# A planned MoE kernel on one core: other orders of the steps in a unit, and GpSimd additions that wait for VectorE sums

## The chip, the cores and the metric

The kernel runs on one core of a Trainium2 chip. The metric is device time in microseconds, the median over runs of the same program; lower is better. The engines are named as in the profile: PE (TensorE matmul), PEld (its weight load), DVE (VectorE), ACT (ScalarE), POOL (GpSimd) and SP (SyncE, which here only starts DMAs).

## The reference

Linear attention with an exponential feature map gives x, 4608 rows of 512 columns. A mixture of eight experts follows; its routing weights P come from eight rounds of row and column normalisation. Only this part is touched by the change:

```python
out = np.zeros((N, D), dtype=np.float32)      # N 4608, D 512
for e in range(E):                            # E 8, F 1024
    h = np.maximum(x @ w1[e], 0.0)
    ye = h @ w2[e]
    out += P[:, e:e + 1] * ye
```

## The kernel before, in words

**Stages.** Attention, routing and expert 0 come first and are not touched. Then experts 1 to 7 follow one another. The 4608 rows are nine groups of 512; x stays in SBUF as xT (bf16) and the result as `acc` (fp32), one tile for each group. Groups are taken in pairs (0,1), (2,3), (4,5), (6,7), and group 8 alone; expert 7 begins with group 8.

**A unit.** For each pair two units are made, one for each value of `fp` (half of the hidden columns); group 8 has one. A unit computes the up product of its own rows, and beside it the down product of an earlier group. Both are done with seven block products in place of eight (Strassen and Winograd's form), so sums of blocks are needed before and after the products:

- Up (`up7`): steps `x1`, `x2`, `x3`, `x4`, `y1`, `w1`, `w2`, each for q = 0 and 1 (`x10` is x1 for q = 0). Each is two wide 128x512 matmuls (L1388) for a pair, and four of 256 columns (L1379) for group 8. `x1` and `x2` are followed by a move, a copy on ACT from one PSUM bank to another (L1447); `w1` by a keep, a copy on ACT to SBUF (L1443); `x3` and `w2` by an addition with relu on DVE (L1450); `y1` and `x4` by a relu on ACT (L1455).
- For pairs of experts 2 to 7 the products x1 and w1 are themselves done with seven inner products: the chains `ia1` to `ia7` (for x1) and `ib1` to `ib7` (for w1), one 128x256 matmul each (L1475). Steps 1 and 2 of a chain are followed by a small copy on ACT (L1484), steps 3 and 4 by a small addition on DVE (`plus`, L1487), which step 4 or 7 of the same chain needs; steps 6 and 7 by the move or keep.
- Down (`down7`): steps `X1`, `X2`, `X3`, `X4`, `Y1`, `Z1`, `Z2`, eight 128x256 matmuls each (L1379). `X1` is followed by a copy to another bank on ACT (L1675). `X2`, `X4` and `Z2` are read by DVE, which adds P times the bank to acc (L1644). `Y1`, `Z1` and `X3` are read by ACT, which scales the bank by P into a buffer V (L1656, two buffers), and POOL adds V to acc (L1659). X1 to X4 use one bank, so that X3 has to be read before X4 begins.
- Sums of blocks are DVE operations on bf16 (L1211): of the weights of each expert (`sums_up`, `inner_sums`, `sums_down`; 128x1024 and 128x256), of the hidden blocks for each down product (`down7`, 128x512), and in expert 1 of x itself (`sums_x`, `inner_x`), which SP stores to DRAM as `xd` and loads again (`X<-xd`) for every later expert. In expert 1 ACT also scales what expert 0 left in acc (L1666).

**What sets the order.** No instruction is issued where it stands in the code. Each call records an `Op` with a cost, its reads and writes; `Plan.schedule` then goes through the recorded operations as a list scheduler: of all operations that are ready it takes the one that can start first, the earlier recorded one on a tie, so the strings `ORDER` and `INNER` set both dependences and priority. The plan holds one more rule: an operation marked `shared` (a DVE sum of blocks, a POOL operation) starts after the last `shared` one has ended (`port`). `Plan.run` then issues the operations in that order, and every engine works through its own in order; across engines only true data dependences are semaphores on the chip. The rule on `shared` lives in the plan alone.

Of the kernel before, what the change touches and what calls it, by code (L numbers as in the profile page):

```python
# [17 lines left out]
class Buf:  # L18


    def __init__(self, ring):
        self.ring, self.t, self.slot, self.left, self.end = ring, None, None, 0, 0.0
        self.last = None
# [91 lines left out]

class Op:
    __slots__ = ("eng", "dur", "lat", "nbytes", "fn", "left", "ready", "users", "idx", "end",
                 "bufs", "deps", "shared", "turn", "unit", "stop", "tiled")

    def after(self, user):  # L120

# [77 lines left out]
class Plan:  # L199
# [3 lines left out]
    def __init__(self):  # L203
        self.last, self.readers = {}, {}
        self.ops = []
        self.prio = 0
        self.port = 0.0

    def op(self, eng, dur, lat, fn, r=(), w=(), takes=(), nbytes=0, shared=False):


        o = Op()
        o.eng, o.dur, o.lat, o.fn, o.nbytes = eng, dur, lat, fn, nbytes
        o.users, o.idx, o.end, o.ready = [], len(self.ops) + self.prio, None, 0.0
        o.shared, o.turn, o.unit, o.tiled = shared, False, 0, 0
        deps = {}
        for key in r:
            for d in self.last.get(key, ()):
                deps[id(d)] = d
        for key in w:  # L220
            for d in list(self.last.get(key, ())) + self.readers.get(key, []):
                deps[id(d)] = d
        bufs = list(takes)
        for key in list(r) + list(w):
            b = key[0] if isinstance(key, tuple) else key
            if isinstance(b, Buf):
                bufs.append(b)
        o.bufs = list({id(b): b for b in bufs}.values())
        for b in o.bufs:
            b.left += 1  # L230
        for key in r:
            self.readers.setdefault(key, []).append(o)
        for key in w:
            self.last[key] = [o]
            self.readers[key] = []
        o.deps = list(deps.values())
        o.left = len(o.deps)
        for d in o.deps:
            d.users.append(o)
        self.ops.append(o)  # L240
        return o

    def start(self, o, free):

        t = max(free, o.ready, self.port if o.shared else 0.0)
        need = {}
        for b in o.bufs:
            if b.slot is None:
                key = id(b.ring.free)
                n = need[key] = need.get(key, 0) + 1  # L250
                at = b.ring.find(n)
                if at is None:
                    return None
                t = max(t, at)
            elif b.last is not None and b.last.eng != o.eng:
                t = max(t, b.last.end)
        return t

    def schedule(self):
        ready = {}  # L260
        free = {}
        links, clock = Links(), Clock()
        for o in self.ops:
            if o.left == 0:
                ready.setdefault(o.eng, []).append(o)
        done = []

        def finish(o):
            for b in o.bufs:
                if b.ring.psum:  # L270
                    b.last = o
                b.left -= 1
                b.end = max(b.end, o.end)
                if b.left == 0:
                    b.ring.give(b.end, b.slot)
            for u in o.users:
                u.left -= 1
                u.ready = max(u.ready, o.after(u))
                if u.left == 0:
                    ready.setdefault(u.eng, []).append(u)  # L280

        while len(done) < len(self.ops) or links.next():
            best = None
            for eng, rq in ready.items():
                f = free.get(eng, 0.0)
                if best is not None and f > best[0]:
                    continue
                for o in rq:
                    t = self.start(o, f)
                    if t is not None and (best is None or (t, o.idx) < best[:2]):  # L290
                        best = (t, o.idx, o)
            landed = links.next()
            if landed and (best is None or landed[0] <= best[0]):
                o = links.land(*landed)
                o.end = landed[0] + 1.0
                finish(o)
                continue
            assert best is not None, "no operation can start"
            at, _, o = best
            ready[o.eng].remove(o)  # L300
            for b in o.bufs:
                if b.slot is None:
                    b.slot = b.ring.take(at)
            dur = clock.takes(at, o.dur, o.tiled) if o.eng == "PE" else o.dur
            free[o.eng] = at + dur
            if o.shared:
                self.port = at + dur
            done.append(o)
            if o.nbytes:
                links.add(o, at)  # L310
            else:
                o.stop = at + dur
                o.end = o.stop + o.lat
                finish(o)
        return done

    def run(self, tc):
        done = self.schedule()
        with tc.manual_schedule():
            for o in done:  # L320
                o.fn()


@with_exitstack
def kernel(
# [159 lines left out]
    def load_w(e, r=()):  # L485
        w1, w2 = new("w1"), new("w2")
        for w, src in ((w1, moe_w1), (w2, moe_w2)):
            dma("POOL", 2 << 20, 280, lambda w=w, src=src: nc.gpsimd.dma_start(
                out=w(), in_=src[e].rearrange("(c p) f -> p c f", p=128)),
                r, [(w, i, j) for i in range(2) for j in range(2)])  # L490
        return w1, w2
# [569 lines left out]
    def stage_g(b):  # L1061
# [4 lines left out]
    at = [0]  # L1066
# [6 lines left out]
    order = (  # L1073
        "lraeaepqbwlqaqawwabwmqlltnrbppnwqbppmrmanbqaqmwwacmpnpbccpwbtcnmqnaqbclupunm"
        "taumquglcapalbcpnqqdcenmucugbblnapmrcqdutabnqpmunpbambccddnqplanmqmducpblttb"
        "augnaqlnrbdcampcadmqeutunqcppmdcaqtdqabpbbmlrqtdnpmuaqualbnagnacctbmqulupran"
        "tdpmtdqcmdnpdabdancpcabbqmpumqbcdgnappqunburqcbugmmnqdcdanumupqbnucmcpnmbddp"
        "bqmpncncubncmmgccg"
    )
# [25 lines left out]
    o = plan.op("X", 0.0, 0.0, swap, w=["late"])  # L1105
# [478 lines left out]
    def down7(e, g, H, B7):  # L1584
# [122 lines left out]


    ORDER = "X1 x10 w10 x11 X2 x20 y10 x21 Z1 y11 X3 w11 x30 x31 x40 x41 w20 Y1 w21 X4 Z2".split()
    INNER = ("ib1 ia1 ia2 ib2 ib3 ia3 X1 Z1 ib5 ia4 ib4 ia5 ia6 ib6 y10 X2 x20 ia7 X3 x21 ib7 "  # L1710
        "x31 y11 w20 x30 Z2 x40 x41 Y1 X4 w21").split()
    END = "X1 p2 Y1 X2 Z1 p3 X3 Z2 X4 p0 p1".split()
    slots, wait = list(range(6)), []

# [20 lines left out]
    for e in range(1, E):  # L1735
        w1, w2 = load_w(e, ["late", ("acc", 4, 0, 0)] if e > 1 else ["late"])
        if e == 1:
            nextX = sums_x(pairs[0])
        A7 = sums_up(e, w1)
        B7 = sums_down(e, w2) if e > 1 else None  # L1740
        turn = [*pairs, (8,)] if e < E - 1 else [(8,), *pairs]
        for n, gs in enumerate(turn):
            X = nextX if e == 1 else load_x(gs)
            H = {g: [] for g in gs}
            for fp in range(len(gs)):
                hs = take()
                for i, z in enumerate(hs):
                    H[gs[min(i, len(gs) - 1)]].append(z)
                un = up7(A7, gs, fp, X, H, ["up0"])
                for o in INNER if ("ia", 1) in un or ("ib", 1) in un else ORDER:  # L1750
                    if o[0] not in "XYZ":
                        un[o[:2], int(o[2])]()
                    elif dn is not None:
                        dn[o]()
                if dn is not None:
                    dn["out"]()
                    slots.extend(dn["slots"])
                if e == 1 and fp == 0 and n:
                    inner_x(turn[n - 1], [(H[gs[0]][0], 0, 1, 1)])
                if e == 1 and fp == 0 and n + 1 < len(turn):  # L1760
                    nextX = sums_x(turn[n + 1], [(H[gs[0]][0], 0, 1, 1)])
                if B7 is None and fp:
                    B7 = sums_down(e, w2)
                if fp == len(gs) - 1:
                    wait += [(e, g, H[g], B7, w2, [z.ring.number for z in H[g]]) for g in gs]
                dn = next_down()
# [35 lines left out]
```

## Time and profile before

| what | value |
|---|---|
| runs, us | 1028.99, 1028.57, 1026.66 (median 1028.57) |
| profiled execution, us | 1027.38 |
| its span, first to last instruction, us | 1025.3 |
| TensorE clock granted | 1.00 |
| DVE busy in the span | 849.4 us (83%) |
| POOL additions L1659 | 186, median 1269 ns, shortest 1260, longest 2078 |
| PE matmul 128x256, mean ns of one | 272 or 273 |
| PE matmul 128x512, mean ns of one | 379 |
| X<-xd loads, median us to landing | 2.7 |
| weight loads on POOL's queue (wx), median us to landing | 12.7 |

How to read it: the span is what the profile shows of one execution, and the time has about 2 us more around it. An expert from 2 on takes some 109 us. Matmuls overlap: the row of one lasts longer than it holds PE, so busy PE in the profile covers a part of each small gap. In a timeline, the bracket at a line's end gives the idle time of its engine before it and the instruction that ended the idle time.

### The profile page before, as it was taken

The numbers are of one execution on the slowest core, as the hardware profiler recorded it, in microseconds if no ns is written. First come the engines' busy times: TensorE is split into PE (matmuls) and PEld (weight loads), VectorE is DVE, ScalarE is ACT, GpSimd is POOL, SyncE is SP. The second block draws the span as 40 slices with busy tenths as digits, with TensorE's granted clock in tenths as the row PEclk, the third lists the DMA queues.
The fourth block names the chain that finished last, engine by engine and source line by source line (L and its number), as shares of the span: only waits on it lengthen the run. The fifth ranks groups of instructions, "written<-read, shape, count | busy, mean of one in ns | idle before, by whom it ended". The sixth has DMA issues, their size and how long they took to land.

```text
span 1025.3 us, 22492 instructions
## 1 busy us (share of the span) xinstructions
PE 1001.4 (98%) x8232; PEld 712.2 (69%) x8232; DVE 849.4 (83%) x1979; ACT 799.8 (78%) x1786; POOL 385.7 (38%) x418
## 2 busy tenths in 40 slices
PE   7899999999999999999999999999999999999998
PEld 4666666644566867787777767786778777786775
DVE  8999989986888997779877887798778977788775
ACT  7999999846878677777777777767776787777874
POOL 5778764400224423343333333333333323323332
PEclk9999999999999999999999999999999999999999
DMA  9999988150113511162116112431126111513343
GB/s 248 193 187 185 175 141 125 34 112 10 48 41 81 122 47 48 47 136 56 48 47 118 40 51 56 82 85 48 47 53 139 47 47 47 109 53 88 135 156 132
DMA packets 115086, 93.94 MB, mean 92 GB/s; under 512 B 54432, under 2 KB 97440, under 8 KB 114976
## 3 DMA queue, kind: packets, MB, share of 16 engines
q1 hardware_dynamic: 83024, 68.46, 26.2%
q0 software_dynamic: 31648, 23.86, 16.5%
q8 instruction: 64, 1.05, 0.4%
q14 instruction: 46, 0.38, 0.1%
q10 hardware_dynamic: 304, 0.20, 0.1%
HBM read 92.62 MB, written 14.55 MB: 105 GB/s over the span
## 4 chain that ended last, share of the span: by engine, by line
PE 91%; DVE 5%; ACT 3%; DMA 1%; issue 1%; SPq 0%; DVEq 0%; ACTq 0%
PE ps L1379 39%; PE ps L1388 24%; PE ps L593 18%; PE ps L1475 7%; PE ps L876 2%; DVE hx L1211 1%; DMA acc<-in_q_dram 1%; DVE hs L1450 1%; ACT k L589 1%; ACT q L589 1%; DVE acc L1644 1%; DVE m L585 0%; ACT hx L1656 0%; DVE hs L1211 0%; DVE wx L585 0%
## 5 line engine op out<-in xcount | busy, mean ns | idle before, releaser
L1659 POOL TENSOR_TENSOR acc<-acc,hx 128x512 f32<-128x512 f32 x186 | 241.9, 1301 | 562.4 <-ACT hx L1656 561.6
L1379 PEld LDWEIGHTS <-hs 128*128 128x128 bf16 x1984 | 193.7, 98 | 59.9 <-issue 2.6
L1450 DVE CUSTOM_DVE_ANT_0 hs<-ps,U 128x512 bf16<-128x512 f32 x252 | 164.7, 684 | 60.6 <-PE ps L1388 57.1
L1644 DVE SCALAR_TENSOR_TENSOR acc<-ps,P,acc 128x256 f32<-128x256 f32 x372 | 163.4, 476 | 40.3 <-PE ps L1379 36.7
L1455 ACT ACTIVATE hs<-ps 128x512 bf16<-128x512 f32 x252 | 151.3, 606 | 57.4 <-PE ps L1388 51.6
L1656 ACT ACTIVATE hx<-ps,P 128x256 f32<-128x256 f32 x372 | 157.8, 479 | 38.5 <-PE ps L1379 34.2
L1379 PEld LDWEIGHTS <-hx 128*128 128x128 bf16 x1488 | 145.5, 98 | 30.5 <-issue 0.2
L1447 ACT COPY ps<-ps 128x512 f32<-128x512 f32 x252 | 146.8, 592 | 25.3 <-PE ps L1475 9.7
L1379 PE MATMUL ps<-hx,hs 128*128 128x256 bf16 x992 | 134.4, 272 | 1.9 <-ACT hx L1656 1.6
L1388 PE MATMUL ps<-X,T 128*128 128x512 bf16 x448 | 131.0, 379 | 1.2 <-DMA X<-xd 1.2
L1388 PEld LDWEIGHTS <-T 128*128 128x128 bf16 x672 | 65.7, 98 | 51.9 <-issue 2.2
L1487 DVE TENSOR_TENSOR ps<-ps,U 128x256 f32<-128x256 f32 x192 | 76.0, 425 | 19.6 <-PE ps L1475 13.3
L1379 PE MATMUL ps<-wx,hs 128*128 128x256 bf16 x560 | 79.5, 273 | 0.0
L1443 ACT COPY U<-ps 128x512 f32<-128x512 f32 x126 | 74.8, 593 | 3.1 <-PE ps L1475 2.7
L1379 PE MATMUL ps<-wx,hx 128*128 128x256 bf16 x496 | 73.9, 273 | 0.0
L593 PE MATMUL ps<-xT,w 128*128 128x512 bf16 x288 | 72.9, 379 | 0.0
L593 PE MATMUL ps<-w,hx 128*128 128x512 bf16 x288 | 72.8, 379 | 0.0
L1379 PE MATMUL ps<-hx 128*128 128x256 bf16 x496 | 70.5, 273 | 0.0
L1388 PE MATMUL ps<-xT,T 128*128 128x512 bf16 x224 | 67.3, 379 | 0.0
L1379 PE MATMUL ps<-w,hx 128*128 128x256 bf16 x432 | 66.5, 273 | 0.0
L1484 ACT COPY ps<-ps 128x256 f32<-128x256 f32 x96 | 32.1, 360 | 38.5 <-PE ps L1475 25.7
L585 DVE TENSOR_REDUCE m<-ps 128x4 f32<-128x512 f32 x88 | 58.7, 678 | 3.8 <-PE ps L593 2.0
(168 smaller groups left out, 1941.6 us busy)
## 6 DMA issues: line engine op xcount, KB each, us to landing
X<-xd SPq DMA_DIRECT2D x72, 256.0 KB, 2.7
wx<-in_moe_w_dram POOLq DMA_DIRECT2D x8, 1024.0 KB, 12.7
v_m<-in_v_dram SPq DMA_DIRECT2D x15, 512.0 KB, 5.5
out_dram<-acc SPq DMA_DIRECT2D x14, 512.0 KB, 3.0
w<-in_moe_w_dram POOLq DMA_DIRECT2D x6, 1024.0 KB, 11.7
XI<-xd SPq DMA_DIRECT2D x24, 192.0 KB, 2.4
qk<-in_k_dram POOLq DMA_DIRECT2D x12, 256.0 KB, 5.4
qk<-in_q_dram POOLq DMA_DIRECT2D x12, 256.0 KB, 6.7
```

Source lines behind the costliest of these rows:

```text
L593: nc.tensor.matmul(out_, lhsT=lhsT, rhs=rhs, start=start, stop=stop)
L1379: pe(256, lambda i=i, k=k, z=z: nc.tensor.matmul(bank()[:, 256 * i:256 * i + 256], lhsT=lhs(k, i), rhs=rhs(k), start=first and z, stop=k = ...
L1388: pe(512, lambda k=k: nc.tensor.matmul(bank().rearrange("p (a b) -> p a b", a=2), lhsT=lhs(k), rhs=rhs(k), start=first and k == 0, stop=k ...
L1443: act(512, lambda: nc.scalar.copy(out=u[q]().rearrange("p a b -> p (a b)"), in_=w[q]()), bk(w[q]), [u[q]])
L1447: act(512, lambda: nc.scalar.copy(out=to[q](), in_=x[q]()), bk(x[q]), [to[q]])
L1450: dve(515, lambda: nc.vector._custom_dve(ADD_SAT, out=out_(q, i, j), in0=bank[q]().rearrange("p (a b) -> p a b", a=2), in1=u[q](), s0=3.0e ...
L1455: act(512, lambda: nc.scalar.activation(out=out_(q, i, j), in_=bank[q]().rearrange("p (a b) -> p a b", a=2), func=ACT.Relu, bias=0.0, scal ...
L1475: pe(256, lambda: nc.tensor.matmul(at(i, h)(), lhsT=blocks[lhs]()[:, fp], rhs=rhs(), start=start, stop=True, skip_group_check=True), [*xal ...
L1487: dve(256, lambda: nc.vector.tensor_tensor(out=at(i, h)(), in0=at(1, 0)(), in1=s(), op=ALU.add), [k[1, 0], (p5, n)], [k[i, h]])
L1644: dve(320, lambda n=n, ts=ts: nc.vector.scalar_tensor_tensor(out=acc[g][:, ts, 256 * j:256 * j + 256], in0=bank()[:, 256 * n:256 * n + 256 ...
L1656: act(370, lambda n=n: nc.scalar.activation(out=u()[:, n, :], in_=bank()[:, 256 * n:256 * n + 256], func=ACT.Copy, bias=0.0, scale=P[:, 4 ...
L1659: pool(695, lambda: nc.gpsimd.tensor_tensor(out=acc[g][:, 2 * i:2 * i + 2, 256 * j:256 * j + 256], in0=acc[g][:, 2 * i:2 * i + 2, 256 * j: ...
```

## The change

Three things. In units with inner chains the string `INNER` has another order. In expert 1, which has no inner chains, the units use a new string `EARLY` in place of `ORDER`; group 8 of the later experts keeps `ORDER`. And a POOL operation is tied to a DVE one: when the plan places a POOL operation, it starts no earlier than the planned end, with latency, of the last `shared` DVE operation placed ahead of it; if it is planned to start within 1.5 us of that operation's stop, it gets a semaphore wait on it (`behind`). A DVE sum planned after a POOL operation gets no wait. Of the additions L1659, 120 get the wait. The operations, their operands and their buffers are the same.

```diff
-        self.port = 0.0
+        self.port, self.vector = 0.0, None
...
         t = max(free, o.ready, self.port if o.shared else 0.0)
+        if o.eng == "POOL" and o.shared and self.vector:
+            t = max(t, self.vector.end)
...
             if o.shared:
                 self.port = at + dur
+                if o.eng == "DVE":
+                    self.vector = o
+                elif self.vector and at < self.vector.stop + 1.5:
+                    o.behind = self.vector
...
             for o in done:
-                o.fn()
+                o.ins = o.fn()
+                if o.behind:
+                    tc.add_manual_dep(
+                        o.ins.ins, o.behind.ins.ins.name, mybir.DependencyInfo(
+                            mybir.DependencyClass.Sync, mybir.DependencyReason.DATA),
+                        reason="order at the shared port")
...
-    INNER = ("ib1 ia1 ia2 ib2 ib3 ia3 X1 Z1 ib5 ia4 ib4 ia5 ia6 ib6 y10 X2 x20 ia7 X3 x21 ib7 "
-        "x31 y11 w20 x30 Z2 x40 x41 Y1 X4 w21").split()
+    INNER = ("ib1 ia1 ib2 ib3 X1 ia2 ia3 ia5 ia6 ib5 x20 ib6 ia4 x30 ia7 x40 ib4 x21 X2 y10 "
+        "ib7 Z1 x31 X3 w20 Z2 y11 w21 x41 Y1 X4").split()
+    EARLY = ("w10 x10 X1 w11 y10 x11 x20 Z1 x30 w20 x21 X2 Y1 x31 w21 X3 Z2 X4 x41 y11 x40").split()
...
-                for o in INNER if ("ia", 1) in un or ("ib", 1) in un else ORDER:
+                for o in INNER if ("ia", 1) in un or ("ib", 1) in un else EARLY if e == 1 else ORDER:
```

What the scheduler makes of the strings, in the order of PE's instructions, for one unit of expert 4 (group pair 4, fp 1; a number is matmuls of 256 columns, a wide one counted as two). Before:

```
ib1*1 ia1*1 ia2*1 ib2*1 X1*8 Z1*3 ia3*1 Z1*1 ib3*1 Z1*4 X2*1 ia4*1 ia5*1 ia6*1 ib5*1 ib4*1 ib6*1 X2*7 ia7*1 Z2*1 y10*4 x20*4 ib7*1 X3*8 x21*4 y11*4 w20*4 x30*4 Z2*2 x31*4 Z2*5 x40*4 Y1*2 x41*4 Y1*6 X4*8 w21*4
```

After:

```
X1*3 ib1*1 ia1*1 ib2*1 X1*5 Z1*1 ia2*1 ia3*1 ia5*1 Z1*2 ib3*1 ib5*1 Z1*2 X2*5 ib6*1 ib4*1 X2*1 ia6*1 ia4*1 X2*2 Z1*2 ib7*1 Z1*1 Y1*1 ia7*1 Y1*1 x20*4 y10*4 X3*2 x21*4 x30*4 X3*6 w20*2 x31*2 x40*4 x31*2 w20*2 Z2*8 y11*4 w21*4 x41*4 Y1*6 X4*8
```

For the first unit of the second pair in expert 1, before and after:

```
x10*4 w10*4 x11*4 x20*4 y10*4 w11*4 x21*4 y11*4 x30*4 w20*2 x31*4 w20*2 w21*4 Z1*8 x40*4 X1*8 x41*4 Z2*7 X2*8 Y1*8 Z2*1 X3*8 X4*8
w10*4 x10*4 w11*4 x11*4 y10*4 x20*4 x21*4 Z1*8 x30*2 X1*8 x30*2 w20*4 x31*4 w21*4 X2*8 Y1*8 Z2*6 X3*8 Z2*2 x41*4 y11*4 x40*2 X4*8 x40*2
```

For the first unit of expert 2, whose first `ib` and `ia` products use the weight sums of the new expert, after (a prime marks a step recorded with the next unit):

```
Z1*8 X1*8 Z2*8 X2*7 ib1*1 ib2*1 X2*1 Y1*8 Z1'*1 ib3*1 ib5*1 Z1'*1 ia1*1 ia2*1 X3*7 ib6*1 ib4*1 X3*1 ia3*1 ia5*1 Z1'*4 ib7*1 Z1'*2 ia6*1 ia4*1 X4*5 ia7*1 X4*3 x20*4 y10*4 x21*4 y11*4 x30*4 w20*4
```

More of the change, by code (lines that the diff above doesn't have):

```diff
@@ L117 @@
     __slots__ = ("eng", "dur", "lat", "nbytes", "fn", "left", "ready", "users", "idx", "end",
-                 "bufs", "deps", "shared", "turn", "unit", "stop", "tiled")
+                 "bufs", "deps", "shared", "turn", "unit", "stop", "tiled", "ins", "behind")
     def after(self, user):
@@ L215, in op @@
         o.shared, o.turn, o.unit, o.tiled = shared, False, 0, 0
+        o.ins = o.behind = None
         deps = {}
```

## The prediction

> **What bounds the kernel now.** I read the page first, then the busy time of the engines in stretches, then who TensorE (PE) waited for, then the timeline around each of those waits.
>
> ```profile
> PE 1001.4 (98%) x8232; PEld 712.2 (69%) x8232; DVE 849.4 (83%) x1979; ACT 799.8 (78%) x1786; POOL 385.7 (38%) x418
> ...
> PE 91%; DVE 5%; ACT 3%; DMA 1%; issue 1%; SPq 0%; DVEq 0%; ACTq 0%
> ```
>
> PE is the bound: the chain that ended last is 91% PE. The change gives PE no fewer matmuls (the built program of each version has the same operations), so it can only win or lose idle time of PE. The stretches show how much there is (columns: PE, PEld, DVE, ACT, POOL busy with counts, then clock, DMA share, GB/s).
>
> ```profile
> 262.00:300.00 38.00, 35.09 (x240) 23.29 (x239) 33.04 (x80) 31.59 (x64) 9.86 (x8) 1.00 0.14 49
> ...
> 350.00:362.00 12.00, 10.30 (x80) 7.58 (x79) 10.15 (x31) 7.79 (x19) 4.57 (x3) 1.00 0.21 68
> ...
> 470.00:579.00 109.00, 108.24 (x834) 81.19 (x832) 89.84 (x211) 83.24 (x186) 36.56 (x29) 1.00 0.30 67
> ```
>
> A whole expert (109 us) has 0.8 us of idle PE; the start of expert 1 has 2.9 and the passage to expert 2 has 1.7. By the waits of PE, first in 262 to 362 us, then in 362 to 1010 us:
>
> ```profile
> PE ps L1379 <- ACT hx L1656: 1.6, 2, 1.2
> PE ps L1475 <- DVE ps L1487: 1.6, 3, 0.7
> PE ps L1388 <- DVE hs L1450: 1.2, 1, 1.2
> ...
> PE ps L1475 <- DVE ps L1487: 3.8, 5, 0.8
> PE ps L1388 <- DMA X<-xd: 1.2, 1, 1.2
> ```
>
> The 3.8 us are one wait of 0.76 us in each of the experts 2 to 6. One of them on the timeline, and the durations of the same VectorE sum elsewhere:
>
> ```profile
> 375.93 1.34 POOL L1659 TENSOR_TENSOR acc<-acc,hx 128x512 f32<-128x512 f32 x1 [3.10 <-ACT hx L1656]
> 376.06 1.75 DVE L1211 TENSOR_TENSOR hx<-w,hx 128x1024 bf16<-128x1024 bf16 x1
> 379.60 0.27 PE L1475 MATMUL ps<-xT,w 128*128 128x256 bf16 x1 [0.76 <-DVE ps L1487]
> ...
> L1211 DVE TENSOR_TENSOR T<-wx 128x1024 bf16<-128x1024 bf16 x9 | 6.2, 684 | 0.0
> L1211 DVE TENSOR_TENSOR hx<-w,hx 128x1024 bf16<-128x1024 bf16 x3 | 5.3, 1755 | 0.0
> ```
>
> The addition began 0.13 us ahead of the sum, and the sum took 1.75 us where its kind takes 0.68: it was held until the addition ended at 377.27. The 1.07 us lost on VectorE passes through L1644, L1450 and L1487 to the next inner matmul. A wait's true price is from start to start: a 128x256 matmul holds PE 0.11 us ((1.03-0.27)/7, from a row of eight in 1.03 us) though its row lasts 0.27, so 0.16 us of idleness hides under the row and 0.76 is 0.92 us.
>
> **The change part by part.** Below a "slot" is that 0.109 us; a wide 128x512 matmul is two. A hand-over PE to VectorE or ScalarE and back costs, by rows, 0.16 (tail) + 0.09 (a matmul's row ends at 376.44, ScalarE's copy of it begins at 376.53) + its own row + 0.06 (L1487 ends at 379.54, its matmul begins at 379.60).
>
> *(a) The wait of the addition.* In the built order 120 of 186 additions gain it, and the two after the big sums of each new expert are among them. Then the sum runs at 0.68 and the addition begins at about 376.74, ending 378.0 in place of 377.27. Behind it on GpSimd stand the next addition (idle 2.9 us before it) and the weight loads, 12.7 us to landing for a use an expert later; the two buffers V that ScalarE's L1656 fills are next wanted at 379.23. So 1.2 us of cover, and nothing is paid; without cover each such addition would cost up to 0.74. Gain 5 x 0.92 = 4.6 us; bounds 0 and 4.6.
>
> The Trainium skill, SBUF — State Buffer, "Who interferes with whom", says that a VectorE instruction with two SBUF inputs and a GpSimd one that reads SBUF exclude each other, whoever begins second being blocked until the first ends; the row of 1.75 agrees. It speaks against the change in so far as a one-sided wait leaves the other meeting open: a delayed addition may hold the next sum for its whole 1.27 us. As an estimate from that rule, twelve such meetings, a tenth of the 120 held additions, would cost VectorE 12 x 1.27 = 15 us; were none of it covered, the sum below would end 6 us above the old time and not 9 below it.
>
> *(b) Expert 1's own order.* Three stalls on the timeline around 273.8, 286.5 and 295.4 us, with one at 271.5:
>
> ```profile
> 271.53 1.03 PE L1379 MATMUL ps<-hx,hs 128*128 128x256 bf16 x8
> 272.80 0.91 ACT L1656 ACTIVATE hx<-ps,P 128x256 f32<-128x256 f32 x2
> 273.76 0.93 PE L1379 MATMUL ps<-hx,hs 128*128 128x256 bf16 x7 [1.20 <-ACT hx L1656]
> ...
> 293.21 1.42 POOL L1659 TENSOR_TENSOR acc<-acc,hx 128x512 f32<-128x512 f32 x1 [5.33 <-ACT hx L1656]
> 293.43 1.35 DVE L1211 TENSOR_TENSOR XI<-xT,XI 128x256 bf16<-128x256 bf16 x1
> 295.44 0.59 PE L1388 MATMUL ps<-X,wx 128*128 128x512 bf16 x2 [1.18 <-DVE hs L1450]
> ```
>
> Start to start they are 0.26 + 1.36 + 0.60 + 1.34 = 3.56 us. The second is X4 directly behind X3 on one bank: no slots between, 1.36 needed. In the new program 12 slots (1.31) stand there. The third had 5 slots (0.55) and lacked 0.60, so it needs 1.15; the new order has 12. The first had 9 slots (0.98) and needs 1.24; it gets 14. The fourth is the collision of (a) again: a 0.28 us sum held to 1.35. So 0.05 is left of all four. New is that in three units y10 follows x11 with no or two slots of other work: its move (0.59) queues behind keep(0) (0.59), so x10 to y10 needs 0.16 + 0.09 + 0.59 + 0.06 = 0.90 against 8 slots = 0.87, plus up to 0.2 of queue; x21 after it likewise. I take 0.5 (bounds 0.1 and 3 x 0.6). Net gain 3.0.
>
> *(c) Expert 2's first unit, 354 to 360 us:* stalls of 0.13, 0.43, 0.29, 0.07, 0.79 and 0.84 = 2.54 us. The addition at 352.50 ran 2.08 us among the small sums (collision), and the ladder ia3, plus, ia4, plus, ia7 needs 0.16 + 0.09 + 0.42 + 0.06 = 0.73 per rung, more when L1644 (0.48) stands ahead. The new order gives 9 and 5 slots to the rungs of ia and 12 and 7 to those of ib: only 5 slots (0.55) is short, by 0.18 to 0.66. I take 0.6 left, gain 1.9 (bounds 0 and 2.5).
>
> *(d) Scattered single stalls* at 422, 657, 702, 760, 873 and 932 us, 0.37 + 0.20 + 0.19 + 0.17 + 0.21 + 0.38 = 1.52 by the starts of successive matmuls, four of them on VectorE. Nothing in the diff aims at one of them, but held sums are among what makes VectorE late: I take half, 0.8 (bounds 0 and 1.5).
>
> *(e) The new INNER in its 48 units.* Some links get shorter. x30 to x40 waits for L1450 (0.69): 0.16 + 0.09 + 0.69 + 0.06 = 1.00 against 10 slots = 1.09 (before 11 slots); x20 to x30 comes to 0.90 against 1.09 (before: over 20 slots); ia4 to ia7 0.73 against 7 slots = 0.76 (before 12). x31 to x41 gets looser (11 slots to 18). X1 to X2 had 10 slots before and has 10 now, and did not stall. So most links just hold, with 0.03 to 0.2 to spare: I charge 0.02 per unit, 1.0 us. Bounds: 0, and L1644's row of 0.48 less the spare 0.1 in every unit, 0.37 x 48 = 18 us.
>
> *(f) The last expert's wait for X* (945.1, 1.36 start to start): eight stores of acc, 0.78 each, stand ahead of the load on SP's queue in both programs, in the same order. A store waits for the additions of its rows, which (a) puts off by up to 0.74, so: 0 (bounds: gain 1.4, loss 0.74).
>
> Sum: -4.6 - 3.0 - 1.9 - 0.8 + 1.0 = -9.3. The profiled execution took 1027.38 us (span 1025.3 and 2.1 around it), so 1018.1. The median of the three runs lies 1.2 above it, the lowest 0.7 below; I take the mean of the four, 1027.9, and forecast 1018.5.
>
> **The rivals.**
> - *Slower: the short links stall in every unit.* VectorE is 82% busy in an expert (89.84 of 109). If L1450 finds an L1644 ahead of it in each unit, 18 us are paid: 1027.9 - 10.3 + 18 = 1035.6. It decides from 10.3/48 = 0.21 us per unit on. Against it: the old order had X1 to X2 at 10 slots, x31 to x41 at 11, and its experts idle 0.8 us, all of it named. Chance 0.08.
> - *Only the wait pays:* the new orders trade their old stalls for new ones, b to e together nothing: 1027.9 - 4.6 = 1023.3. For it: (b) and (c) lie where VectorE and ScalarE carry extra sums and scalings that no order takes away. Chance 0.12.
> - *No effect:* the sums are met from the other side, or arrive as late, so the 0.92 us stays and the orders cancel: 1027.9. Against it: all five stalls have the same pair, sum behind addition. Chance 0.04.
> - The forecast has 0.76.
>
> The range: below, all of a to d, and f, with nothing lost: 1027.9 - 4.6 - 3.6 - 2.5 - 1.5 - 1.4 = 1014.3; above, the second rival with 1.2 of spread, 1024.5. A measurement tells 0.2% (2 us) from no change: faster 0.87, same 0.05, slower 0.08.
>
> **What would show it.** For (a): no L1211 of 1.75 us, no 0.76 wait in experts 2 to 6, additions that name a VectorE sum as releaser. For (b), (c): PE idle in 262 to 300 from 2.9 to about 0.6, at the passage to expert 2 from 1.7 to about 0.5. For (e): experts at 108.1 instead of 109 us; many waits of L1388 on L1450 or L1447 would prove me wrong, as would L1656 waiting for GpSimd. For (f): the X wait still there.

## The result, and the profile after

The changed kernel took 1015.4 us (median of 4 runs, 1014.99 to 1016.64), the kernel before beside it 1027.82: ratio 0.9881, 95% interval 0.9864 to 0.9898, 12.4 us less. The profiled execution has a span of 1013.9 us against 1025.3. New lines stand 12 further down: L1211 is now L1223, L1379 L1391, L1388 L1400, L1450 L1462, L1475 L1487, L1644 L1656, L1656 L1668, L1659 L1671.

The page of the changed kernel: busy time by engine, and the chain that ended last.

```profile
PE 998.8 (99%) x8232; PEld 714.0 (70%) x8232; DVE 853.0 (84%) x1979; ACT 797.5 (79%) x1786; POOL 379.7 (37%) x418
...
PE 94%; ACT 3%; DVE 1%; DMA 1%; issue 0%; DVEq 0%
```

Its stretches (PE, PEld, DVE, ACT, POOL busy, then clock, DMA share, GB/s), at the start of expert 1, at the passage to expert 2, and over one whole expert:

```profile
257.00:295.00 38.00, 37.90 (x251) 24.30 (x249) 33.42 (x81) 32.06 (x65) 9.25 (x8) 1.00 0.17 62
...
345.00:357.00 12.00, 11.96 (x103) 9.77 (x101) 11.19 (x35) 8.60 (x21) 5.04 (x4) 1.00 0.29 85
...
464.00:572.00 108.00, 108.00 (x834) 81.40 (x832) 90.51 (x212) 83.19 (x187) 35.87 (x29) 1.00 0.28 68
```

PE's idle time is gone: 0.1 us where 2.9 stood, 0.04 for 1.7, and an expert takes 108 us and not 109, with the same 834 matmuls. VectorE is no less busy (853.0 us against 849.4). From 350 to 1000 us the waits of PE come to one line, which was there before with 1.2:

```profile
PE ps L1400 <- DMA X<-xd: 1.9, 1, 1.9
```

The place of the former collision on the timeline, the big sum and the addition after it:

```profile
371.73 0.69 DVE L1223 TENSOR_TENSOR hx<-w,hx 128x1024 bf16<-128x1024 bf16 x1
372.56 1.27 POOL L1671 TENSOR_TENSOR acc<-acc,hx 128x512 f32<-128x512 f32 x1 [2.16 <-DVE hx L1223]
```

The sum takes 0.69 and not 1.75, and the addition names it as what it waited for. All 186 additions now last 1.258 to 1.282 us, where the longest was 2.08. But sums are still held by additions, and more of them: counting L1223 rows over 0.05 longer than is usual for their shape (0.29, 0.43, 0.70 us for 256, 512, 1024 columns), 36 of 652 in place of 12, 16.6 us of VectorE in place of 8.9. None of the 36 is followed by a wait of PE on VectorE in this profile. So the meetings did not end, and the profile alone does not say why they stopped costing time. That is what the experiments are for.

### The profile page after: what moved, and what is told of

Read it like the earlier page. It is cut to its first block, busy times and chain, and to the rows that moved or that the text cites. A ratio compares the mean times of both kernels' runs of the same rounds, so it can differ in the third digit from the quotient of the medians.

```text
span 1013.9 us, 22512 instructions
## 1 busy us (share of the span) xinstructions
PE 998.8 (99%) x8232; PEld 714.0 (70%) x8232; DVE 853.0 (84%) x1979; ACT 797.5 (79%) x1786; POOL 379.7 (37%) x418
## 4 chain that ended last, share of the span: by engine, by line
PE 94%; ACT 3%; DVE 1%; DMA 1%; issue 0%; DVEq 0%
PE ps L1391 42%; PE ps L1400 25%; PE ps L605 18%; PE ps L1487 7%; PE ps L888 2%; ACT k L601 1%; ACT q L601 1%; DMA X<-xd 0%; DVE m L597 0%; PE ps L735 0%; DMA acc<-in_k_dram 0%; DVE wx L597 0%; PE ps L917 0%; ACT kr L601 0%; ACT wx L601 0%
## 5 line engine op out<-in xcount | busy, mean ns | idle before, releaser
L1671 POOL TENSOR_TENSOR acc<-acc,hx 128x512 f32<-128x512 f32 x186 | 235.9, 1269 | 556.9 <-ACT hx L1668 295.6
L1391 PEld LDWEIGHTS <-hs 128*128 128x128 bf16 x1984 | 194.1, 98 | 55.9 <-issue 0.4
L1462 DVE CUSTOM_DVE_ANT_0 hs<-ps,U 128x512 bf16<-128x512 f32 x252 | 167.3, 687 | 47.7 <-PE ps L1400 29.9
L1668 ACT ACTIVATE hx<-ps,P 128x256 f32<-128x256 f32 x372 | 161.2, 482 | 46.9 <-PE ps L1391 43.9
L1656 DVE SCALAR_TENSOR_TENSOR acc<-ps,P,acc 128x256 f32<-128x256 f32 x372 | 163.6, 478 | 30.5 <-PE ps L1391 29.2
L1391 PEld LDWEIGHTS <-hx 128*128 128x128 bf16 x1488 | 145.5, 98 | 27.4 <-issue 0.6
L1391 PE MATMUL ps<-hx,hs 128*128 128x256 bf16 x992 | 142.1, 273 | 0.0
L1400 PE MATMUL ps<-X,T 128*128 128x512 bf16 x448 | 131.5, 379 | 1.9 <-DMA X<-xd 1.9
L1400 PEld LDWEIGHTS <-T 128*128 128x128 bf16 x672 | 65.7, 98 | 49.4 <-issue 2.6
L1391 PE MATMUL ps<-wx,hs 128*128 128x256 bf16 x560 | 81.6, 273 | 0.0
L1391 PE MATMUL ps<-wx,hx 128*128 128x256 bf16 x496 | 76.3, 273 | 0.0
L1391 PE MATMUL ps<-hx 128*128 128x256 bf16 x496 | 75.7, 273 | 0.0
L1400 PE MATMUL ps<-xT,T 128*128 128x512 bf16 x224 | 72.4, 379 | 0.0
L1391 PE MATMUL ps<-w,hx 128*128 128x256 bf16 x432 | 69.8, 273 | 0.0
L1391 PE MATMUL ps<-w,hs 128*128 128x256 bf16 x432 | 64.7, 273 | 0.0
## 6 DMA issues: line engine op xcount, KB each, us to landing
wx<-in_moe_w_dram POOLq DMA_DIRECT2D x8, 1024.0 KB, 12.4
```

Source lines behind the costliest of these rows:

```text
L1391: pe(256, lambda i=i, k=k, z=z: nc.tensor.matmul(bank()[:, 256 * i:256 * i + 256], lhsT=lhs(k, i), rhs=rhs(k), start=first and z, stop=k = ...
L1400: pe(512, lambda k=k: nc.tensor.matmul(bank().rearrange("p (a b) -> p a b", a=2), lhsT=lhs(k), rhs=rhs(k), start=first and k == 0, stop=k ...
L1462: dve(515, lambda: nc.vector._custom_dve(ADD_SAT, out=out_(q, i, j), in0=bank[q]().rearrange("p (a b) -> p a b", a=2), in1=u[q](), s0=3.0e ...
L1656: dve(320, lambda n=n, ts=ts: nc.vector.scalar_tensor_tensor(out=acc[g][:, ts, 256 * j:256 * j + 256], in0=bank()[:, 256 * n:256 * n + 256 ...
L1668: act(370, lambda n=n: nc.scalar.activation(out=u()[:, n, :], in_=bank()[:, 256 * n:256 * n + 256], func=ACT.Copy, bias=0.0, scale=P[:, 4 ...
L1671: pool(695, lambda: nc.gpsimd.tensor_tensor(out=acc[g][:, 2 * i:2 * i + 2, 256 * j:256 * j + 256], in0=acc[g][:, 2 * i:2 * i + 2, 256 * j: ...
```

## The experiments

Two theories: the wait pays (theory 1), or the orders pay (theory 2). Three things can be set apart: the rule in the plan (an addition is planned no earlier than the end of the last sum), the waits on the chip, and the two strings. Runs of the kernel before, made beside each group of experiments, had medians of 1027.83, 1028.44 and 1027.74; the ratios are to these.

| run | rule in the plan | waits | INNER | expert 1 | us | ratio to before, 95% |
|---|---|---|---|---|---|---|
| before | no | 0 | old | ORDER | 1027.8 | |
| wait_old_plan | no | 151 | old | ORDER | 1021.5 | 0.9941 (0.9927 to 0.9956) |
| wait_only | yes | 148 | old | ORDER | 1025.1 | 0.9975 (0.9965 to 0.9985) |
| wait_early | yes | 146 | old | EARLY | 1023.5 | 0.9953 (0.9938 to 0.9968) |
| wait_inner | yes | 121 | new | ORDER | 1018.7 | 0.9905 (0.9889 to 0.9922) |
| after | yes | 120 | new | EARLY | 1015.4 | 0.9881 (0.9864 to 0.9898) |
| hold_tight | yes | 74 | new | EARLY | 1016.2 | 0.9877 (0.9863 to 0.9892) |
| no_sem | yes | 0 | new | EARLY | 1023.3 | 0.9964 (0.9949 to 0.9979) |
| orders_only | no | 0 | new | EARLY | 1037.4 | 1.0098 (1.0082 to 1.0115) |
| wait_new_plan0 | no | 123 | new | EARLY | 1033.2 | 1.0056 (1.0041 to 1.0071) |

**The waits alone, in the old program.** wait_old_plan has the kernel before, instruction for instruction in its order; only waits are added. Against the changed kernel it has the old INNER, ORDER for expert 1, and not the rule in the plan:

```diff
-        if o.eng == "POOL" and o.shared and self.vector:
-            t = max(t, self.vector.end)
...
-    INNER = ("ib1 ia1 ib2 ib3 X1 ia2 ia3 ia5 ia6 ib5 x20 ib6 ia4 x30 ia7 x40 ib4 x21 X2 y10 "
-        "ib7 Z1 x31 X3 w20 Z2 y11 w21 x41 Y1 X4").split()
+    INNER = ("ib1 ia1 ia2 ib2 ib3 ia3 X1 Z1 ib5 ia4 ib4 ia5 ia6 ib6 y10 X2 x20 ia7 X3 x21 ib7 "
+        "x31 y11 w20 x30 Z2 x40 x41 Y1 X4 w21").split()
...
-                for o in INNER if ("ia", 1) in un or ("ib", 1) in un else EARLY if e == 1 else ORDER:
+                for o in INNER if ("ia", 1) in un or ("ib", 1) in un else ORDER:
```

> The kernel before, its instructions in its own order on every engine, with 151 waits added: an addition that the old plan starts within 1.5 us of a sum's stop waits for that sum. Nothing is planned anew. Theory 1 (the wait alone ends the harmful meetings where the plan has the sum ahead): the five waits of 0.92 us go and the times fall by 3 to 6 us, 1022 to 1025. Rival (the old plan puts an addition ahead of the sum it hurts, or leaves a held addition no room): within 2 us of before, 1026 to 1029.

Measured 1021.5, 6.3 below before: theory 1, a little beyond its 3 to 6. The sum and addition of the same unit on the timeline:

```profile
375.42 0.68 DVE L1221 TENSOR_TENSOR hx<-w,hx 128x1024 bf16<-128x1024 bf16 x1
376.25 1.27 POOL L1669 TENSOR_TENSOR acc<-acc,hx 128x512 f32<-128x512 f32 x1 [3.96 <-DVE hx L1221]
```

And all waits of PE from 262 to 1000 us (total, count, longest):

```profile
PE ps L1389 <- ACT hx L1666: 1.6, 2, 1.2
PE ps L1485 <- DVE ps L1497: 1.6, 3, 0.7
PE ps L1398 <- DMA X<-xd: 0.9, 1, 0.9
PE ps L1398 <- DVE hs L1460: 0.4, 2, 0.2
```

The 3.8 us of five waits on the inner additions are gone and the wait on `hs` of expert 1 fell from 1.2 to 0.2; the 1.6 and 1.6 of expert 1 and of the passage to expert 2 stand as they were. By starts of successive matmuls that is 5 x 0.92 and 1.34 less 0.27: 5.7 of the 6.3 us. No new wait of PE appeared, so the delayed additions cost nothing that shows there. Of the 12 sums that were held before, the six that go are the five of 1.75 us and the one at 293.43, all ahead of a wait of PE; the other six stay held, and four new ones come.

**Rule and waits with the old strings.**

The changed kernel with INNER as before and ORDER for expert 1, the last two pieces of the diff above.

> The new rule in the plan and its waits, with the old INNER, and ORDER for expert 1 as before. Theory 1 (the wait itself ends the collisions that reached PE): the five waits of 0.92 us in experts 2 to 6 and the collisions at 293 and 352 us go, the orders' own stalls of expert 1 (0.26 + 1.36 + 0.60) stay: 4.6 + 1.3 + 1 = some 7 us below before, about 1021. Theory 2 (the gain needs an order that suits the rule): the old INNER keeps or moves its stalls, 0 to 3 us below before, 1025 to 1028.

Measured 1025.1, the value of theory 2. It is 3.6 us worse than the waits in the old plan. The rule moves additions in the plan, and the scheduler then makes another order of PE's instructions of the same strings (854 of 8232 places differ from the kernel before). The third unit of an expert, on PE:

```profile
482.84 0.27 PE L1487 MATMUL ps<-xT,wx 128*128 128x256 bf16 x1
482.95 0.27 PE L1487 MATMUL ps<-xT,T 128*128 128x256 bf16 x1
483.06 0.27 PE L1487 MATMUL ps<-xT,wx 128*128 128x256 bf16 x1
483.17 0.27 PE L1487 MATMUL ps<-xT,T 128*128 128x256 bf16 x1
...
484.02 0.27 PE L1487 MATMUL ps<-XI,T 128*128 128x256 bf16 x1 [0.57 <-ACT U L1496]
484.59 0.27 PE L1487 MATMUL ps<-XI,T 128*128 128x256 bf16 x1 [0.20 <-ACT U L1496]
485.41 0.83 PE L1391 MATMUL ps<-wx,hx 128*128 128x256 bf16 x6 [0.23 <-DVE hx L1223]
```

Four inner matmuls stand in a row, nothing else between, and the next waits for the copies. With 0.16 hidden under each row the three waits are 0.74, 0.36 and 0.39 us, in four of the experts: 6.0 us in all, as much as the collisions that went.

**The strings one at a time, under the rule.**

Each has one of these two pieces: wait_inner is the changed kernel with ORDER for expert 1, wait_early the changed kernel with INNER as before.

> Rule, waits and the new INNER; expert 1 keeps ORDER. With the rule and waits alone PE still stood still, from start to start, 0.74 + 0.36 + 0.39 = 1.49 us at the third unit of experts 3 to 6, some 6 us in all, and 1.6 us in expert 1 and 2.5 us at the passage to expert 2. Theory 1 (under the rule each order pays for its own place): INNER takes the 6 us and a part of the passage: 1018 to 1020. Theory 2 (the two orders only pay together): 1023 or above.

> Rule, waits and EARLY for expert 1; INNER as before. Theory 1: only expert 1's 1.6 us and a part of the 2.5 us at the passage to expert 2 are won over rule and waits alone (1025.1): 1022 to 1024; with the gain of the run with INNER the two add up to the changed kernel's 1015.4 within 1.5 us. Theory 2: no gain over 1025.

Measured 1018.7 and 1023.5, both in the range of theory 1. From 1025.1, INNER gives 6.4 and EARLY 1.6; together they should give 1017.1, and the changed kernel has 1015.4, a miss of 1.7 where 1.5 was allowed. These runs stand in different groups. Each against its own kernel before, the versions lie 2.7 (wait_only), 9.8 and 4.9 us below it; so INNER gives 7.1, EARLY 2.2, and with the 2.7 that makes 12.0 of the 12.4. INNER's gain is clear of the noise. EARLY's is not by time alone: its interval overlaps that of wait_only, and that of wait_inner overlaps that of the changed kernel. The traces show it. There, INNER takes the waits shown above; the passage to expert 2 is EARLY's: its gaps of 0.15 us or more add up to 2.4 us with wait_inner and to 0.5 with wait_early.

**The changed program without its waits.** Same instructions, same order on every engine; only the waits are left out.

```diff
-                if o.behind:
+                if False:
```

> The changed kernel with the same instructions in the same order on every engine; only the 120 waits are left out. Theory 1: additions again start as soon as ScalarE is done, hold sums that PE waits for, and a part of the 12.4 us is given back: 2 to 8 us above the changed kernel, 1017 to 1023. Theory 2 (the order is the whole of it): 1015.4 within 1 us.

Measured 1023.3 (1021.0 to 1028.9 over ten runs): 7.9 us are given back, at the upper end of theory 1. Here is one place, first with the waits, then without them. (The profile without waits is of the longest of the ten executions; it is already 5.7 us behind when expert 1 begins, ahead of this place.)

```profile
452.01 0.29 DVE L1223 TENSOR_TENSOR T<-wx,T 128x256 bf16<-128x256 bf16 x1
...
452.22 1.88 DVE L1462 CUSTOM_DVE_ANT_0 hs<-ps,U 128x512 bf16<-128x512 f32 x3
452.47 2.60 POOL L1671 TENSOR_TENSOR acc<-acc,hx 128x512 f32<-128x512 f32 x2 [2.20 <-DVE T L1223]
...
453.61 0.60 PE L1391 MATMUL ps<-X,w 128*128 128x256 bf16 x4
```

```profile
458.94 1.26 POOL L1671 TENSOR_TENSOR acc<-acc,hx 128x512 f32<-128x512 f32 x1 [1.93 <-ACT hx L1668]
459.04 1.32 DVE L1223 TENSOR_TENSOR T<-wx,T 128x256 bf16<-128x256 bf16 x1
...
460.28 1.87 DVE L1462 CUSTOM_DVE_ANT_0 hs<-ps,U 128x512 bf16<-128x512 f32 x3
...
461.61 0.60 PE L1391 MATMUL ps<-X,w 128*128 128x256 bf16 x4 [0.80 <-DVE hs L1462]
```

With the waits the addition begins after the sum `T<-wx,T`, which takes 0.29. Without them it slips in front of this sum by 0.10 us; the sum takes 1.32, everything behind it on VectorE is late, and PE waits for L1462. At another place in the changed kernel an addition does hold a sum, and PE does not wait:

```profile
458.53 1.27 POOL L1671 TENSOR_TENSOR acc<-acc,hx 128x512 f32<-128x512 f32 x1 [3.45 <-DVE T L1223]
...
459.09 0.99 DVE L1223 TENSOR_TENSOR hx<-hx,hs 128x512 bf16<-128x512 bf16 x1
```

That sum is the one the plan put behind the addition, so the plan has counted the time. The two whole traces say the same. Without the waits 42 sums are held: 31 of them are among the 36 of the changed kernel, and 11 are not. The plan starts each of the 36 at the end of a POOL operation, and each of the 11 behind another VectorE sum, with the addition later. Each of the nine gaps of PE over 0.3 us between 300 and 1000 us, the wait for X left out, comes within 4 us of the start of one of the 11; the nine add up to 8.2 us. This is the answer to the 36 held sums: here a meeting cost PE time where the plan did not have it, and not where it did.

**How many waits are needed.**

```diff
-                elif self.vector and at < self.vector.stop + 1.5:
+                elif self.vector and at < self.vector.stop + 0.2:
```

> The changed kernel, the same instructions in the same order, but the wait only where the plan starts the addition within 0.2 us of the sum's stop: 74 of the 120 waits. Without any wait the time was 1023.3. Theory 1 (only the additions that directly follow a sum race it): the 74 are enough, 1015 to 1016.5. Rival (VectorE runs late by more than 0.2 us in places, so the wider margin is needed): a part comes back, 1017 to 1021.

Measured 1016.2 (1014.20 to 1016.25), ratio 0.9877 against 0.9881, with PE's instructions in the same order: waits at the 74 additions that are planned directly behind a sum are enough. Whether each of the 74 is needed was not tried.

**The strings without the rule.**

```diff
-                if o.eng == "DVE":
-                    self.vector = o
-                elif self.vector and at < self.vector.stop + 1.5:
+                if self.vector and at < self.vector.stop + 1.5:
```

> The new INNER and EARLY, but the plan without the new rule and without the waits. Theory 1 (the wait is what pays): not better than before in experts 2 to 6, sums held by additions at some points that reach PE; only expert 1's 2.9 us may be won: 1025 or above, at worst over 1030. Theory 2 (the orders pay): within 3 us of the changed kernel, 1015 to 1018.

Then the same program with 123 waits (the changed kernel without the rule in the plan, the first piece of wait_old_plan's diff):

> The new INNER and EARLY planned without the rule, as in the run of the orders alone (1037.4), with 123 waits added and nothing moved. Theory 1 (the orders alone lost to races between additions and sums): most of the 10 us above before comes back, 1020 to 1026. Rival (without the rule the planned order itself is bad, the waits can't mend it): 1033 or above.

Measured 1037.4 and 1033.2. The new strings alone are 10 us slower than before: theory 2 (1015 to 1018) falls, and of theory 1 only its "at worst over 1030" fits. With waits it is the rival's value: waits win back 4.2 and no more. The waits of PE from 257 to 1020 us show which, first without waits, then with them:

```profile
PE ps L1485 <- DVE ps L1497: 5.1, 7, 1.1
PE ps L1485 <- ACT U L1494: 5.1, 7, 1.0
```

```profile
PE ps L1485 <- ACT U L1494: 5.1, 7, 1.0
...
PE ps L1485 <- DVE ps L1497: 1.0, 3, 0.7
```

The wait for VectorE falls by 4.1, and the wait for ScalarE's copies stays at 5.1; that line does not stand among the waits of the changed kernel. The rest is thus the planned order: without the rule the same strings come out as another order on PE. So theory 1 alone is too simple as well: the strings belong to the rule, and the rule to the waits.

**The last wait for X.** In the changed kernel, SP's queue and PE in the last expert:

```profile
924.31 6.18 SPq L1207 DMA_DIRECT2D out_dram<-acc  x8
930.59 1.11 SPq L1341 DMA_DIRECT2D X<-xd  x2
...
934.29 1.02 PE L1400 MATMUL ps<-X,T 128*128 128x512 bf16 x4 [1.89 <-DMA X<-xd]
```

First the eight stores of group 8 were made two of 512 KB:

```diff
-            for i in range(2):
-                b = 2 * ts + i
+            for i in range(2) if ts == 3 else ():
...
-                dma("SP", 1 << 17, 320, lambda b=b, rows=rows: nc.sync.dma_start(
-                    out=out[b * S + SM:(b + 1) * S], in_=acc[8][rows, ts, :]),
-                    [("acc", 8, ts, j) for j in range(2)], [("out", 8, b)])
+                dma("SP", 1 << 19, 320, lambda i=i, rows=rows: nc.sync.dma_start(
+                    out=out.rearrange("(t i s) d -> i s t d", i=2, s=S)[i, SM:S],
+                    in_=acc[8][rows]),
+                    [("acc", 8, t, j) for t in range(4) for j in range(2)], [("out", 8, i)])
```

> The changed kernel with the eight stores of group 8 (128 KB each, 0.78 us each on SP's queue) made into two of 512 KB. Theory: they are what holds the X load of the last expert back, so the X load is issued some 4 us earlier, the wait of PE for X (1.89 us on the changed kernel's timeline, 2.06 from start to start) goes, and the time is 2 us below the changed kernel: 1013.4. Rival: the load waits for its buffer or the link, and the stall stays: 1015.4.

Measured 1015.6, the rival's value: the first load now goes out ahead of the stores, but the second stands behind them.

```profile
924.72 1.36 SPq L1206 DMA_DIRECT2D out_dram<-acc  x2
926.17 1.96 SPq L1341 DMA_DIRECT2D X<-xd  x1
...
933.02 0.60 PE L1400 MATMUL ps<-X,wx 128*128 128x512 bf16 x2 [1.24 <-DMA X<-xd]
```

It was issued at 926.17 and landed 6.8 us later, when PE's wait for it ended, where such a load lands in 2.7 (median). In the changed kernel the two loads were issued only at 930.59 and 931.23, behind 6.2 us of issues, and each landed within 3.7. So with fewer issues the second load went out 5.1 us sooner and landed only 1.9 us sooner. Next, the stores were put behind the loads:

```diff
             X = nextX if e == 1 else load_x(gs)
+            while held:
+                held.pop()()
...
-                    dn["out"]()
+                    (held.append if e == E - 1 and n == 1 and fp else lambda f: f())(dn["out"])
...
-                    [("acc", 8, ts, j) for j in range(2)], [("out", 8, b)])
+                    [("acc", 8, ts, j) for j in range(2)] + ["order of X"], [("out", 8, b)])
```

> The changed kernel with the eight stores of group 8 put behind the two X loads on SP's queue. Two stores of 512 KB ahead of the loads did not pay: the wait for the first load went, but PE then waited 1.24 us for the second one. Theory (it is the bytes of the stores, 1 MB ahead of the load, and not their number on the queue): with the loads ahead both waits go, 2 us below the changed kernel, 1013.4. Rival (the second load is late for its own buffer): 1.2 to 1.4 us of the wait stay, 1014.5 to 1015.4.

> The version with the stores of group 8 behind the X loads again, in more rounds and beside the changed kernel itself: 1.5 to 2.2 us below it (one gap of PE of 2.06 us gone), or, if the order of the stores is no more than chance, the same.

> The changed kernel again, as the yardstick of the run beside it: 1015.4 within 1 us.

Measured 1013.72 (0.9864, 0.9849 to 0.9880), then 1014.05 (0.9868, 0.9853 to 0.9883) beside 1015.99 for the changed kernel measured with it (0.9890, 0.9873 to 0.9906). No wait of PE over 0.2 us is left between 300 and 1000 us but one of 0.20 at the passage. The gain is 1.7 and 1.9 us in the medians, and in the second pair no run of one version reaches a run of the other (1013.24 to 1014.59 against 1014.95 to 1016.60). The intervals of the ratios overlap all the same, so its size is not settled; it is the fastest version measured. In the second profile of the changed kernel this wait is 1.0 and not 2.06, so the wait itself varies.

## Why the prediction was right, point by point

The forecast was 1018.5 with 1014.3 to 1024.5, the measurement 1015.4: direction and range right, the gain 3 us too small (9.3 to 9.4 for 12.4). The three large terms, (a) to (c), came out in size. That the sum came no further off is partly luck: the errors in (d) and (e), 0.55 and 2.0 too little gain, and in (f), 0.7 too much, partly cancel, and the parts do not add up one by one as the sum had it.

- *(a) the wait of the addition,* 4.6: right in cause and size. wait_old_plan shows that the five waits go and no new wait of PE comes. What I didn't see is that the same lines also re-plan: with the old strings the rule gives 3.6 us back (wait_only against wait_old_plan).
- *The sentence on the shared port,* that a delayed addition may hold the next sum: it does. 24 more sums are held and VectorE loses 7.7 us more. That PE would pay for it fell: the plan has the sum behind the addition, with room.
- *(b) expert 1,* 3.0: by the trace the gaps of expert 1 over 0.02 us go from 3.6 to 0.7, so 2.9; the new gaps where y10 follows x11 are 0.26 + 0.13 + 0.09 = 0.5, as charged. But EARLY is only a part of it: the fall of the fourth stall from 1.34 to 0.27 comes with the waits alone, and the third (0.60) is gone in wait_only, with ORDER. Left to EARLY are the stalls of 0.27 and 1.36 that wait_inner still has. The step from wait_inner to the changed kernel is 3.3 us by the medians (2.6 with each against its own kernel before) and 3.3 by the gaps, of which 1.1 lie in expert 1 and 2.2 at the passage.
- *(c) the passage to expert 2,* 1.9: size right (2.54 to 0.5), cause wrong in part. I named the addition at 352.50 among the small sums; with waits alone 2.5 us stay. And it isn't the rungs of the new INNER: EARLY removes it with the old INNER too.
- *(d) scattered waits,* 0.8 for late VectorE: the reason fell. Waits alone leave all six as they were (0.39, 0.21, 0.19, 0.17, 0.22, 0.36); with the new orders 0.17 is left. Gain 1.35.
- *(e) the short links of INNER,* charged 1.0: the step that failed, and in sign. No wait at x30 to x40 or ia4 to ia7 is among the gaps over 0.1 us in whole experts, and the gaps of up to 0.1 us fell by some 0.2 us in an expert, 1.0 in all from routing on. It is INNER's doing: those small gaps add up to 1.6 us in wait_only and to 0.6 in wait_inner. That such links hold because everything around them comes at its planned time is likely and was not tried by itself.
- *(f) the wait for X:* it stayed, 1.36 to 2.06 in the profile, within the bounds given. The stores ahead of the load are the cause: with the loads ahead the wait goes. It is not only their eight issues of 0.78 us, as the run with two of them shows; that it is their bytes is likely and not shown.
- *Rivals.* "Slower" did not come: INNER's links held. "Only the wait pays" (1023.3) lies 1.8 above what the waits alone give (1021.5), and the new strings, with the rule, gave 6 us more. That the orders need the rule and the waits (7.9 us without the waits, 22 without both) stood in none of the rivals; I had priced the parts as if they added up.

By starts of matmuls from routing on, the gaps that went add up: 4.6 (a) + 2.9 (b) + 2.0 (c) + 1.35 (d) + 1.0 (small ones) - 0.7 (f) = 11.1 of the 11.4 us by which the span of the two profiles fell.

## What to carry to other kernels

Where two engines can hold one another, an order that lives only in a plan is a race: here 0.1 us decided which of the two went first, and most of the losses that the plan did not have ran on to PE. Pin the planned order with a wait at those places (74 were enough here), then search the orders again under the same rule, and don't judge an order, or a wait, without the other. The held time that the plan knew cost PE nothing here, so count what the bounding engine waits for, not meetings.

## What the hardware showed that I had not expected

- A held sum isn't simply delayed by the addition: it ends some 0.14 us sooner than the addition's end plus its own usual time. At 376.06 in the kernel before, the addition ended at 377.27, the sum at 377.81 (0.54 later, usual 0.68); at 459.09 above, 459.80 and 460.08 (0.28, usual 0.42).
- The hold goes both ways: in the kernel before an addition took up to 2.08 us where 1.27 is usual, with the waits of the changed kernel at most 1.28. It does not touch every VectorE instruction: L1656, which reads a bank and acc, runs at 0.87 us a pair also while an addition is under way (458.30 to 459.17 in the changed kernel, with the addition from 458.53 on).
- An X load behind 1 MB of stores on the same queue took 6.8 us to land where 2.7 is usual. It need not be the queue: in the changed kernel the three X loads from 437 us on landed in 5.9 to 6.5 us with no store ahead, while two weight loads of 1 MB on POOL's queue were under way (from 432.58 to 447.95). That fits the bytes on the way as the cause, which was not tried by itself.
